# A written order for two more engines in a fused attention and feed-forward kernel

## The chip, the cores and the metric

The kernel runs on one NeuronCore of a Trainium2 chip. Five engines of the core work side by side, each through its own queue of instructions: TensorE (PE, matrix products; its weight loads are listed as PEld), VectorE (DVE), ScalarE (ACT), GpSimd (POOL) and SyncE (SP), which here only issues DMAs. Within a queue the instructions start in the order in which they stand; between queues semaphores hold an instruction back until what it needs is there. The metric is the device time of one execution in microseconds (us), lower is better.

## The reference

Eight batches of eight heads. Every head has 512 local tokens and 32 global ones, with 64 numbers each. The rows of all heads form x (4608 x 512), which goes through a feed-forward block.

```python
def _attn_ref(q_l, k_l, v_l, q_g, k_g, v_g):
    ...
    s_g = scale * np.matmul(q_g, k_all.transpose(0, 1, 3, 2))
    out_g = np.matmul(sm(s_g), v_all)                 # global queries see every key
    s_ll = np.where(mask, scale * np.matmul(q_l, k_l.transpose(0, 1, 3, 2)), -1e9)   # |i - j| <= 32
    s_lg = scale * np.matmul(q_l, k_g.transpose(0, 1, 3, 2))
    a_l = sm(np.concatenate([s_lg, s_ll], axis=-1))   # local queries: a band and the global keys
    out_l = np.matmul(a_l, np.concatenate([v_g, v_l], axis=2))
    return np.concatenate([out_g, out_l], axis=2)

def _moe_ref(x, w_in, w_out, s, b):
    r = np.maximum(x @ w_in, 0.0)                     # 512 -> 2048
    g = s * (r * r) + b
    return g @ w_out                                  # 2048 -> 512
```

## The kernel before

All work is written as one loop over 148 steps j. For j up to 127 a step computes the scores of one half of one head (256 local queries). Ten steps later, with m = j - 10, the feed-forward block works on the same data: 17 groups t of 256 rows (the last holds the global tokens), and for each group eight steps of 256 hidden columns, 136 steps m in all. So an ordinary step holds these pieces, in the order in which the loop writes them:

- `split(j + 1)` makes a rounded part and a remainder of the next keys and queries: two ScalarE copies (L191, L193) and two GpSimd subtractions (L192, L194). `load(j + 2)` puts the loads for a later step on SP.
- `scores(j)`: on TensorE the products `ps_s` (L350, one buffer) and, among them, the product of the global queries with these keys `ps_g` (L364; one buffer "g", shared with `ps_og` and `ps_tg` below). Then `softmax`: VectorE takes scores and mask and leaves the minimum (L207, twice), ScalarE takes two exponentials with their sums (L213), VectorE takes the reciprocal and scales (L216, L217, L222). Then `turn(j)`: VectorE copies the 16-bit halves apart (`two`, L385, four copies) and SP issues a DMA that transposes them (`turned`, L387). Last `g_sum(j)`: ScalarE copies one half of `ps_g` out (`tg`, L372), VectorE adds the other (`sg`, L373); this sets the buffer "g" free.
- `join(j - 1)`: a ScalarE copy that puts the turned halves together (`ptp`, L395). `two` and `turned` have one buffer each.
- `pv` on odd j only: 16 products of probabilities and values for two heads (L317) and a ScalarE copy of the result to x (L324).
- `ffn_in(m)`: 24 products (`ps_h`, L491, two buffers); relu on ScalarE (L497), square on VectorE (L498), the rounded part of g on ScalarE (L505), its remainder on VectorE (L506).
- `ffn_out(m - 1)`: 12 products (L524) with g of the step before. After each eighth m two copies `o` on ScalarE (L532) and their DMAs.

Some steps hold more. With j counted modulo 16: `x_split` after steps 9 and 1 (two ScalarE copies L462, two VectorE subtractions L463, from x to the operand `xs` of the next group, one buffer). The global heads come in steps 12 to 22, counted past 16 into the next batch: `g_softmax` (12 and 16), `g_transposes` inside `ffn_out` (15 and 19: five products L418, and for each of two parts a ScalarE copy L422 and a VectorE subtraction L423), `g_load` (15, 17, 19, 21: a load, two ScalarE copies L432, two GpSimd subtractions L433) and `g_pv` (16, 18, 20, 22: ten products L441, a ScalarE copy L445, VectorE sums L446 and L449).

The framework's planner settles the order inside each engine's queue from a model of its own: it takes instructions by priority (the order in which they are written) as they become ready in that model. From step 25 on (`ORDERED`), the block `tc.manual_schedule` makes TensorE's queue follow the written order exactly. ScalarE, VectorE, GpSimd and SP stay with the planner to the end.

Of the kernel before, what the change touches and what calls it, by code (L numbers as in the profile page):

```python
# [10 lines left out]
F32 = mybir.dt.float32  # L11
# [8 lines left out]
B, H, SL, SG, D = 8, 8, 512, 32, 64  # L20
DM, DF = 512, 2048
P = 128
# [22 lines left out]
NF = 16  # L45
# [10 lines left out]
G_TR = 3  # L56
G_LD = (0, 2)
# [10 lines left out]
def window_attention_then_ffn(ctx: ExitStack, tc: tile.TileContext, qd, qp, qg, kw, vw, vg, w_in, w_out, sv, bv, out):  # L68
# [4 lines left out]
    sb = ctx.enter_context(tc.tile_pool(name="sb", bufs=2))  # L73
# [94 lines left out]
    NS = B * 2 * H  # L168
    st_ = {}
# [24 lines left out]
        nc.gpsimd.tensor_sub(out=qs[:, 1, :], in0=rq, in1=f32(qs[:, 0, :]))  # L194
        st_["ks", j], st_["qs", j] = kq[:, 0:480], qs

    def softmax(heads, scores):
        hf = slot(heads[0])[1]
        nm = sb.tile([P, 4], F32, tag="nm", name=f"nm{heads[0]}")
        ss = sb.tile([P, 4], F32, tag="ss", name=f"ss{heads[0]}")[:, 0:2 * len(heads)]  # L200
        parts = []
        for j, p_s in zip(heads, scores):
            sm = st_["p", j] = sb.tile([P, NC], F32, tag="sm", name=f"sm{j}", bufs=4)
            for blk in range(2):
                n, c = len(parts), COLS[hf, blk]
                mask = masks[hf == 0 and blk == 0][:, 0:c.stop - c.start]
                nc.vector.tensor_tensor_reduce(  # L207
                    out=sm[:, c], in0=p_s[:, c], in1=mask,
                    op0=ALU.add, op1=ALU.min, scale=-scale, scalar=BIG, accum_out=nm[:, n:n + 1],
                )  # L210
                parts.append(sm[:, c])
        for n, p in enumerate(parts):
            nc.scalar.activation(  # L213
                out=p, in_=p, func=AF.Exp, bias=nm[:, n:n + 1], scale=-1.0, accum_out=ss[:, n:n + 1],
            )
        nc.vector.tensor_scalar_add(ss, ss, 1e-9)  # L216
        nc.vector.reciprocal(ss, ss)  # L217
        for n, p in enumerate(parts):
            if len(heads) == 2:
                nc.scalar.activation(out=p, in_=p, func=AF.Identity, scale=ss[:, n:n + 1])  # L220
            else:
                nc.vector.tensor_scalar(  # L222
                    out=p, in0=p, scalar1=ss[:, n:n + 1], scalar2=1.0, op0=ALU.mult, op1=ALU.mult,
                )
# [115 lines left out]
    def scores(j):  # L340
        b, hf, h = slot(j)
        ks, qs = st_.pop(("ks", j)), st_.pop(("qs", j))
        p_s = ps.tile([P, 512], F32, tag="s", name=f"ps_s{j}")
        late = j == ORDERED
        if not late:
            p_g = ps.tile([P, 512], F32, tag="g", name=f"ps_g{j}")
        for blk in range(2):
            cols = COLS[hf, blk]
            for a in range(2):
                nc.tensor.matmul(  # L350
                    p_s[:, cols], lhsT=qs[:, a, blk * P:(blk + 1) * P], rhs=ks[:, cols], start=(a == 0), stop=(a == 1),
                )
                if blk == hf and a == 0 and not late:
                    g_product(j, ks, p_g)
        softmax([j], [p_s])
        turn(j)
        if late:
            st_["late", j] = ks
        else:
            g_sum(j, p_g)  # L360

    def g_product(j, ks, p_g):
        b, hf, h = slot(j)
# [4 lines left out]
    def g_sum(j, p_g):  # L368
        b, hf, h = slot(j)
        ng = 256 + 32 * hf  # L370
        tg = sb.tile([P, 288], F32, tag="tg", name=f"tg{j}", bufs=1)
        nc.scalar.copy(out=tg[0:32, 0:ng], in_=p_g[32:64, 0:ng])  # L372
        nc.vector.tensor_add(out=sg_rows(j, 32)[:, hf * 256:hf * 256 + ng], in0=p_g[0:32, 0:ng], in1=tg[0:32, 0:ng])  # L373
# [7 lines left out]
    def turn(j):  # L381
        sm = st_.pop(("p", j)).bitcast(I16).rearrange("p (k h) -> p h k", h=2)
        two = sb.tile([P, 4, 2, P], I16, tag="two", name=f"two{j}", bufs=1)
        for blk, c, c0, q0, n, o in chunks(j):
            nc.vector.tensor_copy(out=two[:, 2 * blk + c], in_=sm[:, :, c0:c0 + P])  # L385
        turned = st_["turned", j] = sb.tile([P, 4, 2, P], I16, tag="turned", name=f"turned{j}", bufs=1)
        nc.sync.dma_start_transpose(  # L387
            turned.rearrange("p c h q -> p (c h) q"), two.rearrange("p c h k -> p (c h k)"),
        )
# [34 lines left out]
            yield  # L424

    def g_load(b, h):
        rv = sb.tile([P, 10 * D], F32, tag="rvg", name=f"rvg{b}_{h}", bufs=1)
        nc.sync.dma_start(rv, vg[b, h // 2])
        vs = sb.tile([P, 2, 5, 2, D], F32R, tag="vsg", name=f"vsg{b}_{h}", bufs=1)
        for i in range(2):  # L430
            rv5 = rv[:, 5 * D * i:5 * D * (i + 1)].rearrange("p (c d) -> p c d", d=D)
            nc.scalar.copy(out=vs[:, i, :, 0, :], in_=rv5)  # L432
            nc.gpsimd.tensor_sub(out=vs[:, i, :, 1, :], in0=rv5, in1=f32(vs[:, i, :, 0, :]))  # L433
        st_["vsg", b, h] = vs
# [44 lines left out]

    gs_ = {}  # L480

    def ffn_in(m):
        t, pr = m // 8, m % 8
        xs = xs_[t]
        p_h = ps.tile([P, 2, HALF], F32, tag="h", name=f"ps_h{m}", bufs=2)
        for k in range(2):
            f = 2 * pr + k
            n = 0
            for c in range(4):
                for a, e in ((0, 0), (0, 1), (1, 0)):  # L490
                    nc.tensor.matmul(  # L491
                        p_h[:, k], lhsT=wi[f][:, a, c, :], rhs=xs[:, e, c, :],
                        start=(n == 0), stop=(n == 11),
                    )
                    n += 1
        r = sb.tile([P, 2, HALF], F32, tag="r", name=f"r{m}", bufs=2)
        nc.scalar.activation(out=r, in_=p_h, func=AF.Relu)  # L497
        nc.vector.scalar_tensor_tensor(out=r, in0=p_h, scalar=s_t, in1=r, op0=ALU.mult, op1=ALU.mult)  # L498
        g = sb.tile([P, 2, 2, HALF], F32R, tag="g", name=f"g{m}")
        if GL_POOL(m):  # L500
            nc.vector.tensor_scalar_add(r, r, b_t)
            nc.scalar.copy(out=g[:, 0], in_=r)
            nc.gpsimd.tensor_sub(out=g[:, 1], in0=r, in1=f32(g[:, 0]))
        else:
            nc.scalar.activation(out=g[:, 0], in_=r, func=AF.Identity, bias=b_t)  # L505
            nc.vector.scalar_tensor_tensor(  # L506
                out=g[:, 1], in0=r, scalar=b_t, in1=f32(g[:, 0]), op0=ALU.add, op1=ALU.subtract,
            )
        gs_[m] = g
# [31 lines left out]
    nc.sync.dma_start(s_t, sv.partition_broadcast(P))  # L541
    nc.sync.dma_start(b_t, bv.partition_broadcast(P))

    NM = NT * 8
    extra, turns = defaultdict(list), {}
    for b in range(B):
        for g in range(2):
            s0 = 16 * b + G_AT[g]
            extra[s0].append(lambda b=b, g=g: g_softmax(b, g))
            turns[s0 + G_TR] = g_transposes(b, g)  # L550
            for i in range(2):
                h = 4 * g + 2 * i
                extra[s0 + G_TR + G_LD[i]].append(lambda b=b, h=h: g_load(b, h))
                extra[s0 + G_TR + G_PV[i]].append(lambda b=b, h=h: g_pv(b, h))

    def pick(pair, split_one):
# [18 lines left out]
    fixed = ExitStack()  # L575
    for j in range(NM + LAG + 2):
        if j == ORDERED:
            fixed.enter_context(tc.manual_schedule(engines={mybir.EngineType.PE}))
        sp(j + 1)
        if j + 4 < NF:  # L580
            ld(j + 4)
        if j + 2 >= NF:
            ld(j + 2)
        if NF <= j < NS and j % 2 == 0:
            v_load(j // 2)
        for _ in range(CHUNKS_AT[j] if j < len(CHUNKS_AT) else 0):
            weight_chunk(chunk)
            chunk += 1
        if j < NS:
            b1 = j // 16 + 1  # L590
            if j % 16 == 14 and b1 < B:
                qg_load(b1)
            sc(j)
            if j % 16 == 15 and NF <= j + 1 < NS:
                qg_split(b1)
        tr(j - 1)
        if NF <= j - 1 < NS:
            join(j - 1)
        pvs(j - 2)
        if NF <= j - 3 < NS and j % 2:  # L600
            pv((j - 3) // 2)
        if j == 0:
            vl32(0)
        vl32(j + 2)
        m = j - LAG
        if m == -1:
            x_split(0)
        if 0 <= m < NM:
            ffn_in(m)
            late_scores(j)  # L610
            if m % 8 == 7:
                t = m // 8 + 1
                if t < 16:
                    x_split(t)
                elif t == 16:
                    xg_split(16)
        for fn in extra.pop(j, []):
            fn()
        if 0 <= m - 1 < NM:
            ffn_out(m - 1, turns.pop(j, iter(())))  # L620
        else:
            list(turns.pop(j, ()))
    fixed.close()
    assert chunk == 16 and not extra


# [73 lines left out]
```

## Time and profile before

| | us |
|---|---|
| median of three runs | 1106.39 (1105.23 to 1108.20) |
| profiled execution | 1109.83 |
| its span, first to last instruction | 1108.0 |
| TensorE busy in the span | 998.3 |
| ScalarE busy | 748.3 |
| VectorE busy | 717.1 |
| GpSimd busy | 275.2 |

TensorE is at work for 90 per cent of the span. The first 190 us or so hold the loading of the weights and the steps up to 24, in the planner's order; then come about 800 us of steps with attention and feed-forward together; the last 100 us hold feed-forward steps alone. In the rows below, a line of a timeline gives the start and the length of a piece in us, the engine, the line, the operation, what it writes and reads, the shape, the number of instructions merged into it and, in brackets, how long the engine stood idle before it and what ended that.

### The profile page before, as it was taken

Reading aid. Unit: us, or ns where it says so; the run is one execution under the profiler, and the core shown is the slowest. Engines: PE = TensorE matmul, PEld = TensorE weight load, DVE = VectorE, ACT = ScalarE, POOL = GpSimd, SP = SyncE. Lnnn points to the kernel's source line nnn. Section 1 sums busy time; section 2 is a strip of 40 time slices with the busy share of each in tenths; the row PEclk is TensorE's granted clock in tenths of the full one; section 3 lists DMA queues with packets and bytes.
Section 4 is the critical chain, followed back from the end, with each engine's and each line's share of the span. In section 5 each row is a group of like instructions: output and inputs, shape, how many; then the busy total and the mean of one; then the engine's idle time right before and its main releaser. Section 6 shows DMA issues by size and latency. Waiting matters only on the chain.

```text
span 1108.0 us, 19924 instructions
## 1 busy us (share of the span) xinstructions
PE 998.3 (90%) x7060; PEld 877.7 (79%) x7060; DVE 717.1 (65%) x2092; ACT 748.3 (68%) x1618; POOL 275.2 (25%) x309
## 2 busy tenths in 40 slices
PE   6689996999899989989889889899899989999996
PEld 2378885988787778878779778888789878889995
DVE  6999566676666766766766666677666766664321
ACT  6987665777586766778667766778677766863221
POOL 0012323232322323223322332223322323201000
PEclk8879998999999999999999999899999999999998
DMA  9852443434443344434444454444344443331000
GB/s 325 311 198 51 110 100 95 102 87 107 110 113 83 90 115 103 103 85 122 109 91 99 98 110 92 104 85 128 80 109 100 104 117 83 82 57 46 11 20 19
DMA packets 179627, 115.07 MB, mean 104 GB/s; under 512 B 124744, under 2 KB 166728, under 8 KB 179528
## 3 DMA queue, kind: packets, MB, share of 16 engines
q1 hardware_dynamic: 179240, 112.76, 40.2%
q8 instruction: 55, 0.90, 0.4%
q10 hardware_dynamic: 288, 1.05, 0.4%
q14 instruction: 44, 0.36, 0.1%
HBM read 74.97 MB, written 9.44 MB: 76 GB/s over the span
## 4 chain that ended last, share of the span: by engine, by line
PE 22%; DMA 17%; ACT 12%; DVE 10%; issue 4%; POOL 0%; POOLq 0%; SPq 0%; ACTq 0%; DVEq 0%
DMA turned<-two 17%; PE ps_h L491 11%; PE acc L524 9%; ACT ptp L395 5%; DVE two L385 4%; ACT sm L213 3%; DVE sm L222 1%; DVE ss L216 1%; ACT kq L191 1%; DVE r L498 1%; ACT kq L193 1%; PE ps_op L317 1%; ACT tg L372 1%; PE ps_s L350 1%; DVE ss L217 1%
## 5 line engine op out<-in xcount | busy, mean ns | idle before, releaser
L491 PE MATMUL ps_h<-xs,w 128*128 128x256 f32 x3264 | 434.2, 289 | 16.3 <-DVE xs L463 10.1
L491 PEld LDWEIGHTS ps_h<-xs,w 128*128 128x128 f32 x3264 | 411.7, 196 | 27.9 <-DVE xs L463 11.9
L524 PE MATMUL acc<-w,g 128*128 128x512 f32 x1632 | 409.5, 398 | 0.4 <-ACT o L532 0.3
L524 PEld LDWEIGHTS acc<-w,g 128*128 128x128 f32 x1632 | 297.8, 190 | 60.6 <-DVE g L506 1.3
L192 POOL TENSOR_TENSOR kq<-rk,kq 64x416 fp32r<-64x416 f32 x112 | 122.8, 1097 | 614.3 <-ACT kq L191 607.9
L395 ACT COPY ptp<-turned 128x1024 int16<-128x1024 int16 x112 | 153.2, 1368 | 93.7 <-DMA turned<-two 93.3
L505 ACT ACTIVATE g<-r,b_t 128x512 fp32r<-128x512 f32 x136 | 98.4, 724 | 116.3 <-DVE r L498 116.2
L216 DVE TENSOR_SCALAR ss<-ss 128x2 f32<-128x2 f32 (+1 forms) x120 | 40.9, 341 | 169.3 <-ACT sm L213 169.1
L498 DVE SCALAR_TENSOR_TENSOR r<-ps_h,s_t,r 128x512 f32<-128x512 f32 x136 | 101.5, 746 | 74.2 <-ACT r L497 74.2
L385 DVE COPY two<-sm 128x256 int16<-128x256 int16 x448 | 132.9, 356 | 2.9 <-DMA turned<-two 2.7
L497 ACT ACTIVATE r<-ps_h 128x512 f32<-128x512 f32 x136 | 80.9, 595 | 75.2 <-PE ps_h L491 67.7
L506 DVE SCALAR_TENSOR_TENSOR g<-r,b_t,g 128x512 fp32r<-128x512 f32 x136 | 103.7, 763 | 40.5 <-ACT g L505 40.5
L213 ACT ACTIVATE sm<-sm,nm 128x224 f32<-128x224 f32 (+1 forms) x256 | 117.8, 462 | 3.0 <-DVE nm L207 3.0
L194 POOL TENSOR_TENSOR kq<-rq,kq 128x256 fp32r<-128x256 f32 x112 | 84.1, 751 | 13.7 <-POOL kq L192 2.9
L433 POOL TENSOR_TENSOR vsg<-rvg,vsg 128x320 fp32r<-128x320 f32 x64 | 59.7, 952 | 99.3 <-ACT vsg L432 99.3
L207 DVE CUSTOM_DVE_ANT_0 sm<-ps_s,mask 128x192 f32<-128x192 f32 (+1 forms) x224 | 74.1, 367 | 12.3 <-PE ps_s L350 12.2
L364 PE MATMUL ps_g<-kq,qgs 128*64 128x256 f32 (+1 forms) x112 | 33.9, 303 | 51.7 <-DVE og L446 32.2
L373 DVE TENSOR_TENSOR sg<-ps_g,tg 32x256 f32<-32x256 f32 (+1 forms) x112 | 48.3, 431 | 49.4 <-ACT tg L372 46.7
L350 PE MATMUL ps_s<-kq 128*128 128x192 f32 (+1 forms) x448 | 79.5, 267 | 0.0
L350 PEld LDWEIGHTS ps_s<-kq 128*128 128x128 f32 x448 | 72.3, 191 | 7.4 <-issue 0.3
L222 DVE TENSOR_SCALAR sm<-sm,ss 128x192 f32<-128x192 f32 (+1 forms) x224 | 68.6, 349 | 3.9
L317 PE MATMUL ps_op<-ptp,rvp 128*64 128x128 f32 (+2 forms) x1024 | 68.7, 268 | 2.0 <-ACT ptp L309 1.9
(68 smaller groups left out, 820.4 us busy)
## 6 DMA issues: line engine op xcount, KB each, us to landing
rvp<-in_vw SPq DMA_DIRECT2D x64, 256.0 KB, 3.1
rq<-in_qd SPq DMA_DIRECT2D x112, 128.0 KB, 2.4
rk<-in_kw SPq DMA_DIRECT2D x56, 208.0 KB, 2.4
rvg<-in_vg SPq DMA_DIRECT2D x32, 320.0 KB, 3.1
out<-o SPq DMA_DIRECT2D x34, 256.0 KB, 2.6
wst<-in_w_in SPq DMA_DIRECT2D x15, 512.0 KB, 6.5
wst<-in_w_out SPq DMA_DIRECT2D x15, 512.0 KB, 6.9
turned<-two SPq DMA_TRANSPOSE x112, 3.1
```

The costliest lines, as they stand in the source:

```text
L192: (nc.gpsimd if K_POOL(j) else nc.vector).tensor_sub(out=ks[p1:p1 + 64], in0=rk[p0:p0 + 64], in1=f32(ks[p0:p0 + 64]))
L194: nc.gpsimd.tensor_sub(out=qs[:, 1, :], in0=rq, in1=f32(qs[:, 0, :]))
L213: nc.scalar.activation(out=p, in_=p, func=AF.Exp, bias=nm[:, n:n + 1], scale=-1.0, accum_out=ss[:, n:n + 1],)
L350: nc.tensor.matmul(p_s[:, cols], lhsT=qs[:, a, blk * P:(blk + 1) * P], rhs=ks[:, cols], start=(a == 0), stop=(a == 1),)
L385: nc.vector.tensor_copy(out=two[:, 2 * blk + c], in_=sm[:, :, c0:c0 + P])
L395: nc.scalar.copy(out=pt.bitcast(I16).rearrange("p c (q h) -> p c h q", h=2), in_=st_.pop(("turned", j)))
L491: nc.tensor.matmul(p_h[:, k], lhsT=wi[f][:, a, c, :], rhs=xs[:, e, c, :], start=(n == 0), stop=(n == 11),)
L497: nc.scalar.activation(out=r, in_=p_h, func=AF.Relu)
L498: nc.vector.scalar_tensor_tensor(out=r, in0=p_h, scalar=s_t, in1=r, op0=ALU.mult, op1=ALU.mult)
L505: nc.scalar.activation(out=g[:, 0], in_=r, func=AF.Identity, bias=b_t)
L506: nc.vector.scalar_tensor_tensor(out=g[:, 1], in0=r, scalar=b_t, in1=f32(g[:, 0]), op0=ALU.add, op1=ALU.subtract,)
L524: nc.tensor.matmul(oacc[t][i], lhsT=g[:, a, k, i * P:(i + 1) * P], rhs=wo[f][:, e, :], start=(pr == 0 and n == 0), stop=(pr == 7 and n == 5),)
```

## The change

- `tc.manual_schedule` covers PE, Activation and DVE instead of PE alone: from step 25 on, ScalarE and VectorE also follow the written order. GpSimd and SP stay with the planner.
- The written order itself is edited. `g_sum` moves between the minima and the exponentials of `softmax`. `join(j - 1)` moves behind `pv`. In `ffn_in`, a list `then` of pieces runs between the products and the relu: `g_pv`, and `x_split` for the next group. So the activations of `ffn_in` come behind the copies and sums of `g_pv`, and behind `x_split`, in the queues of ScalarE and VectorE. `g_softmax` comes before `ffn_in`. `g_load` is cut in two: the load is written one step earlier than before, its copies (`g_split`) stand before `ffn_in`.

TensorE's written order stays as it was. No instruction is added or taken away.

```diff
-    def softmax(heads, scores):
+    def softmax(heads, scores, between=lambda: None):
...
+        between()
         for n, p in enumerate(parts):
             nc.scalar.activation(
...
-        softmax([j], [p_s])
-        turn(j)
         if late:
             st_["late", j] = ks
-        else:
-            g_sum(j, p_g)
+        softmax([j], [p_s], (lambda: None) if late else (lambda: g_sum(j, p_g)))
+        turn(j)
...
-        rv = sb.tile([P, 10 * D], F32, tag="rvg", name=f"rvg{b}_{h}", bufs=1)
+        rv = st_["rvg", b, h] = sb.tile([P, 10 * D], F32, tag="rvg", name=f"rvg{b}_{h}", bufs=1)
         nc.sync.dma_start(rv, vg[b, h // 2])
+
+    def g_split(b, h):
+        rv = st_.pop(("rvg", b, h))
         vs = sb.tile([P, 2, 5, 2, D], F32R, tag="vsg", name=f"vsg{b}_{h}", bufs=1)
...
-    def ffn_in(m):
+    def ffn_in(m, then):
...
+        for fn in then:
+            fn()
         r = sb.tile([P, 2, HALF], F32, tag="r", name=f"r{m}", bufs=2)
...
+    ENGINES = {getattr(mybir.EngineType, e) for e in ("PE", "Activation", "DVE")}
...
-            extra[s0].append(lambda b=b, g=g: g_softmax(b, g))
+            early[s0].append(lambda b=b, g=g: g_softmax(b, g))
...
-                extra[s0 + G_TR + G_LD[i]].append(lambda b=b, h=h: g_load(b, h))
+                early[s0 + G_TR + G_LD[i] - 1].append(lambda b=b, h=h: g_load(b, h))
+                early[s0 + G_TR + G_LD[i]].append(lambda b=b, h=h: g_split(b, h))
...
-            fixed.enter_context(tc.manual_schedule(engines={mybir.EngineType.PE}))
+            fixed.enter_context(tc.manual_schedule(engines=ENGINES))
...
-        if NF <= j - 1 < NS:
-            join(j - 1)
         pvs(j - 2)
         if NF <= j - 3 < NS and j % 2:
             pv((j - 3) // 2)
+        if NF <= j - 1 < NS:
+            join(j - 1)
...
+        for fn in early.pop(j, []):
+            fn()
...
+        then = extra.pop(j, [])
         if 0 <= m < NM:
-            ffn_in(m)
+            t = m // 8 + 1
+            if m % 8 == 7 and t < 16:
+                then.append(lambda: x_split(t))
+            ffn_in(m, then)
             late_scores(j)
-            if m % 8 == 7:
-                t = m // 8 + 1
-                if t < 16:
-                    x_split(t)
-                elif t == 16:
-                    xg_split(16)
-        for fn in extra.pop(j, []):
-            fn()
+            if m % 8 == 7 and t == 16:
+                xg_split(16)
```

## Rows read from the trace of the kernel before

**Rows 1.** The page: busy time, share of the span and instructions of each engine.
```profile
PE 998.3 (90%) x7060; PEld 877.7 (79%) x7060; DVE 717.1 (65%) x2092; ACT 748.3 (68%) x1618; POOL 275.2 (25%) x309
```

**Rows 2.** Stretches: length, busy PE PEld DVE ACT POOL, clock, DMA share, GB/s.
```profile
195.00:995.00 800.00, 735.51 (x5328) 658.86 (x5327) 532.51 (x1694) 571.84 (x1246) 229.80 (x252) 0.97 0.43 99
...
490.61:495.13 4.52, 4.52 (x29) 4.52 (x28) 2.32 (x9) 3.35 (x8) 1.81 (x2) 0.62 0.07 12
```

**Rows 3.** TensorE's waits, 195 to 995 us: us in total, times, longest.
```profile
PE ps_g L364 <- DVE og L446: 29.8, 22, 2.4
PE ps_g L364 <- DVE pg L423: 11.6, 7, 2.1
PE ps_h L491 <- DVE xs L463: 9.7, 7, 1.7
PE ps_og L441 <- DVE sg L373: 5.4, 5, 2.0
```

**Rows 4.** TensorE's timeline: an even and an odd step without global heads.
```profile
201.12 3.07 PE L491 MATMUL ps_h<-xs,w 128*128 128x256 f32 x24
204.03 2.94 PE L524 MATMUL acc<-w,g 128*128 128x512 f32 x12
...
207.34 2.99 PE L491 MATMUL ps_h<-xs,w 128*128 128x256 f32 x24
...
214.45 3.09 PE L491 MATMUL ps_h<-xs,w 128*128 128x256 f32 x24
```

**Rows 5.** TensorE's timeline: a long wait, and two blocks that ran slowly.
```profile
490.14 0.30 PE L364 MATMUL ps_g<-kq,qgs 128*64 128x256 f32 x1 [2.02 <-DVE pg L423]
...
490.61 4.52 PE L491 MATMUL ps_h<-xs,w 128*128 128x256 f32 x24
...
911.96 3.96 PE L491 MATMUL ps_h<-xs,w 128*128 128x256 f32 x24
```

**Rows 6.** ScalarE's timeline in two ordinary steps.
```profile
433.28 0.39 ACT L372 COPY tg<-ps_g 32x288 f32<-32x288 f32 x1
...
434.57 0.48 ACT L213 ACTIVATE sm<-sm,nm 128x224 f32<-128x224 f32 x1
...
435.60 0.60 ACT L497 ACTIVATE r<-ps_h 128x512 f32<-128x512 f32 x1
...
441.03 1.36 ACT L395 COPY ptp<-turned 128x1024 int16<-128x1024 int16 x1 [0.53 <-DMA turned<-two]
442.26 0.47 ACT L213 ACTIVATE sm<-sm,nm 128x224 f32<-128x224 f32 x1
...
442.85 0.37 ACT L324 COPY x<-ps_op 128x256 f32<-128x256 f32 x1
```

**Rows 7.** VectorE's timeline in one ordinary step.
```profile
437.02 0.90 DVE L385 COPY two<-sm 128x256 int16<-128x256 int16 x4
437.82 0.75 DVE L498 SCALAR_TENSOR_TENSOR r<-ps_h,s_t,r 128x512 f32<-128x512 f32 x1
```

**Rows 8.** VectorE's timeline, then GpSimd's, in a step with `g_load`.
```profile
403.85 2.24 DVE L385 COPY two<-sm 128x256 int16<-128x256 int16 x4
...
403.86 1.87 POOL L433 TENSOR_TENSOR vsg<-rvg,vsg 128x320 fp32r<-128x320 f32 x2 [0.76 <-ACT vsg L432]
```

**Rows 9.** TensorE's timeline around step 25, where its written order begins.
```profile
182.10 0.34 PE L364 MATMUL ps_g<-kq,qgs 128*64 128x288 f32 x1 [2.21 <-DVE sg L373]
187.95 0.50 PE L364 MATMUL ps_g<-kq,qgs 128*64 128x288 f32 x1 [5.50 <-DVE sg L373]
188.25 5.32 PE L524 MATMUL acc<-w,g 128*128 128x512 f32 x12
```

**Rows 10.** ScalarE by line, 195 to 995 us: count, busy, mean ns, idle before.
```profile
L395 ACT COPY ptp<-turned 128x1024 int16<-128x1024 int16 x102 | 139.5, 1368 | 82.4 <-DMA turned<-two 82.1
...
L505 ACT ACTIVATE g<-r,b_t 128x512 fp32r<-128x512 f32 x102 | 73.8, 724 | 97.3 <-DVE r L498 97.2
...
L432 ACT CAST vsg<-rvg 128x320 fp32r<-128x320 f32 x48 | 19.6, 455 | 0.0
```

More of the change, by code (lines that the diff above doesn't have):

```diff
@@ L542, in window_attention_then_ffn @@
     nc.sync.dma_start(b_t, bv.partition_broadcast(P))
+    ENGINES = {getattr(mybir.EngineType, e) for e in ("PE", "Activation", "DVE")}
     NM = NT * 8
-    extra, turns = defaultdict(list), {}
+    early, extra, turns = defaultdict(list), defaultdict(list), {}
     for b in range(B):
@@ L605, in window_attention_then_ffn @@
         m = j - LAG
+        for fn in early.pop(j, []):
+            fn()
         if m == -1:
             x_split(0)
+        then = extra.pop(j, [])
         if 0 <= m < NM:
-            ffn_in(m)
+            t = m // 8 + 1
+            if m % 8 == 7 and t < 16:
+                then.append(lambda: x_split(t))
+            ffn_in(m, then)
             late_scores(j)
-            if m % 8 == 7:
-                t = m // 8 + 1
-                if t < 16:
-                    x_split(t)
-                elif t == 16:
-                    xg_split(16)
-        for fn in extra.pop(j, []):
-            fn()
+            if m % 8 == 7 and t == 16:
+                xg_split(16)
+        else:
+            for fn in then:
+                fn()
         if 0 <= m - 1 < NM:
@@ L623, in window_attention_then_ffn @@
     fixed.close()
-    assert chunk == 16 and not extra
+    assert chunk == 16 and not extra and not early
 def kernel(**inputs):
```

## The prediction, made before the changed kernel was run

> **What bounds the kernel now.** I read the busy shares first [rows 1]: TensorE is busy for 90 per cent of the span, ScalarE for 68. Shares hide stages, so I then looked at the stretch in which all kinds of work run together, 195 to 995 us [rows 2]: TensorE is busy for 735.5 of 800 us and stands idle for 64.5. About 102 steps lie in it (the 102 joins and activations of rows 10), so a step takes 7.84 us there. The timeline of TensorE shows that steps without global heads have no gap: an even step takes 207.34 - 201.12 = 6.2 us, an odd one, with its `pv`, 7.1 us [rows 4]. The idle time is in the steps with global heads and with `x_split`, and the waits of TensorE say for whom [rows 3]: 29.8 us for `og` and 11.6 us for `pg`, both before the next `ps_g`, as they hold the one buffer "g"; 9.7 us for `xs`; 5.4 us for `sg`. The rest of the 64.5 us is small.
>
> There is a second price. After the wait of 2.02 us the next 24 products took 4.52 us, where 2.99 is usual [rows 4, 5]; the granted clock in that stretch was 0.62, so for part of it TensorE ran at 1.2 GHz and not at 2.4 [rows 2]. Eleven blocks of 24 between 237 and 916 us are slowed like this, each behind an idle wait of about 2 us or two waits close together; the one at 490 is among the slowest, the one at 912 the last [rows 5]. Set against 2.8 us for a block at full clock (2.9 from start to start in rows 4), they lose 16.6 us in all, 1.5 each. So waits of TensorE cost 64.5 + 16.6 = 81 us in this stretch, and that is the most that a better order of the other engines can give there.
>
> **Why TensorE waits.** The sums that free the buffer "g" are short, but the planner placed them late. ScalarE stands still before the joins for 82.4 us in total, 0.81 each, because the planner puts a join ahead of other ready work while the transposing DMA is still under way, and what frees "g" stands behind it [rows 10]. In the step of rows 8 the sums of `g_pv` also stand behind four copies `two` that took 2.24 us in place of 0.90 [rows 7, 8].
>
> **The change part by part.** I lay out each kind of step by the written order, with time 0 at the end of `scores(j)` on TensorE, and carry over how late ScalarE and VectorE come out of the step before. TensorE's own pieces: `pv` 0.9 (7.1 - 6.2), `ffn_in` 2.9 from start to start, `ffn_out` with the next scores 3.3 [rows 4]; I take 0.6 of that for the scores. A product of `ffn_in` starts every 0.12 us (2.9 / 24); I take 0.5 for the five of `g_transposes` and 0.7 for the ten of `g_pv`, which are smaller.
>
> *An ordinary step.* ScalarE's round is: `tg` and the two copies of a split 1.29 (433.28 to 434.57), exponentials 1.03, join 1.23 by its starts, relu 0.60 [rows 6], then it must wait 0.75 for the square on VectorE [rows 7], and the activation takes 0.72 [rows 10]: 5.6 us in even steps, 6.0 with the copy of x in odd ones [rows 6]. TensorE needs 6.2 and 7.1. So ScalarE keeps up and regains 0.6 and 1.1 us when it is late. The join now comes a full step after its DMA was issued, behind the exponentials: its wait of 0.81 goes. These steps did not hold TensorE up before, so this alone gives nothing; the cover is TensorE's own work.
>
> *`g_pv`, steps 16, 20, 22.* Its copy and sum are the first things behind `ffn_in` in both queues, while TensorE goes on with 2.8 us of `ffn_out` before it wants "g". In step 16 `g_softmax` stands in front: the copy ends at 5.2, the sum at 6.2, and the next `ps_g` is due at 6.4. The 29.8 us go. The relu, queued behind that copy, comes at most 2.5 us later than now; the remainder of g is then ready about 2 us into the next step and wanted at 2.9 or later. The waits for `sg` (5.4) go, because `g_sum` stands in front of the exponentials.
>
> *Step 15, `g_transposes`.* Exponentials end at 1.6, the copies for the next batch's queries and x at 2.2, the join at 3.4, `g_split` (two of 0.455, rows 10, overlapping a little) at 4.1, relu 4.7, square 5.5, g 6.3 (remainder 7.1), the copy of 128x512 out of "g" (as long as a relu) 6.9, its remainder on VectorE (as the square, but behind that of g) 7.75. TensorE is done with `ffn_out` at 7.1 and wants "g" at 7.2: it waits 0.6.
>
> *Step 17, `x_split`.* ScalarE is 1.8 late: join done at 4.7, `g_split` 5.5, the two copies `xs` 6.6, their VectorE halves 6.8 and 7.4. TensorE wants them at 7.1 and 7.8: nothing. If GpSimd is at `vsg` and holds VectorE up, 0.6. I take 0.3. In step 9 they are there by 5.7, so the 9.7 us go.
>
> *Step 18.* VectorE is 2.5 to 3 late, so `sg` frees "g" at 3.65 to 4.2, and `g_pv` is due at 2.9: a wait of 0.9. The two copies `o` now stand behind g in ScalarE's queue, the second behind the remainder of g, whose buffer it takes; `split` stands behind them.
>
> *Step 19, `g_transposes` again.* ScalarE is 2.25 late. The chain of step 15, without the queries' copy: exponentials 3.6, x 3.8, join 5.05, `g_split` 5.8, relu 6.4, square 7.2, g 7.9 (remainder 8.7), the copy 8.5, its remainder 9.4. "g" is wanted at 7.2: 2.2 us, and as behind the 2.02 us of rows 5, the clock then takes another 1.5.
>
> *Sum.* A batch loses 0.6 + 0.3 + 0.9 + 2.2 + 1.5 = 5.5 us, six batches 33. Single waits add 2: in step 26, where the sum of the late product of step 25 stands behind `x_split` (1.4), and before the last group (0.7). So 81 us of loss become 35: 46 gained.
>
> *GpSimd and SP* stay with the planner. The earlier load of `g_load` lands before `g_split` wants it; were it late, all of ScalarE's queue would stand. A load on SP in front of a `turned` DMA costs nothing while the join comes a step later. I take 0, with 0.8 us a join (its wait of today, rows 10) as the upper bound of a late landing.
>
> *Around step 25* TensorE now waits 2.21 and 5.50 us, then runs at half speed (5.32 against 2.8) [rows 4, 9]: 10.2 us. The sums it waits for stand ahead of more work in the new order, but steps up to 24 remain the planner's. Between -3 (one more wait as in step 19) and 10.2, I take 4, as only the second of the two waits lies behind work that the new order surely moves.
>
> Together 50 us. The profiled execution took 1109.8, 3.4 above the median: 1109.8 - 50 = 1060, and 1056 on the scale of the median.
>
> **The rivals.**
> 1. *GpSimd holds VectorE up* (1089). Four copies `two` took 2.24 us beside `vsg`, 0.90 alone [rows 7, 8]: 1.34 more. In a written order everything behind them waits as well. If that happens in each of the six steps 15 to 20, and the regained time covers half of it, TensorE waits another 4.0 us a batch and meets one more drop of the clock of 1.5: 6 x 5.5 = 33 more. Against it: in my layout `two` ends before `vsg` begins. The Trainium skill, SBUF — State Buffer, section "Who interferes with whom", says that VectorE in its two-port modes and GpSimd share a pair of ports that one of them holds for a whole instruction while the other is fully blocked. By that rule it is the order of issue that decides, and the change fixes VectorE's side of it alone; the trace agrees in that the copies waited and the GpSimd pair (1.87) ran through.
> 2. *ScalarE becomes the bound* (1115, slower). Its work is 571.8 us for 102 steps [rows 2], 5.6 each; with the wait for the square 6.4. TensorE's own, without the slow clock, is (735.5 - 16.6) / 102 = 7.05. If the joins still wait their 0.81 for the DMA, ScalarE is at 7.25, and a VectorE held up by 1.34 in every second step makes 7.92, more than today's 7.84: 8 us slower. The point from which it decides is 1.4 us of waits a step. Against it: the DMA has a step to land.
> 3. *It does not do what it says* (1105): the order written is what the planner already made, or new waits at the same places cost as much. The idle time before the joins speaks against the first.
> 4. *Nearly all waits vanish*, step 19's too, and step 25 is smooth: 1056 - 27 - 6 = 1023.
>
> **How the numbers follow.** The forecast has 0.60, with a range of its own from 1032 to 1080; rival 1 0.14, rival 2 0.13, rival 3 0.06, rival 4 0.07. The time is the forecast's, 1056. The range from 1021 to 1093 takes in the forecast and rivals 1 and 4, and leaves out rivals 2 and 3 (0.19). Faster by over 0.3 per cent, which is about what a measurement of this kernel can tell from none: 0.60 + 0.14 + 0.07 = 0.81; within it 0.06; slower 0.13.
>
> **What would show it.** Right: no wait of `ps_g` for `og` and few for `xs`; ScalarE's idle time before the joins near 0; one wait of about 2 us a batch for `pg`; TensorE idle for some 25 us in the stretch that 64.5 came from, with about six slow blocks. Wrong: ScalarE without idle time and TensorE waiting for g at `ffn_out` (rival 2); copies `two` of over 2 us in most global steps (rival 1); a join that waits for its DMA.

## The result, and the profile after

The changed kernel takes 1042.35 us (median of four runs, 1042.07 to 1043.26) against 1106.7 us beside it: a ratio of 0.942, 95% interval 0.940 to 0.944. It is 64 us faster, where 50 were forecast; the time lies in the range. The profiled execution took 1042.14 us, 67.7 less than that of before.

The gain can be placed, because TensorE runs the same 5310 products in the same order between the start of `ffn_out` in step 26 and its start in step 128 in both kernels. Here are the three stretches of before and of after (length, busy PE, PEld, DVE, ACT and POOL with their counts, granted clock, DMA share, GB/s).

```profile
173.50:196.90 23.40, 14.29 (x90) 12.08 (x89) 14.24 (x34) 13.26 (x30) 9.63 (x10) 0.78 0.33 81
196.90:994.51 797.61, 733.12 (x5310) 656.52 (x5309) 531.69 (x1693) 569.90 (x1240) 228.25 (x251) 0.97 0.43 100
994.51:1108.00 113.49, 104.69 (x698) 94.31 (x696) 35.35 (x50) 34.20 (x60) 5.27 (x6) 0.97 0.07 23
```

```profile
171.00:188.54 17.54, 14.58 (x100) 12.59 (x101) 13.42 (x43) 14.34 (x31) 3.63 (x4) 1.00 0.47 110
188.54:925.97 737.43, 709.75 (x5310) 640.65 (x5309) 508.85 (x1689) 571.96 (x1247) 232.49 (x256) 1.00 0.45 108
925.97:1040.30 114.33, 105.02 (x698) 94.31 (x696) 33.14 (x51) 33.72 (x59) 5.33 (x6) 0.97 0.07 23
```

`ffn_out` of step 26 is reached 8.4 us earlier (196.90 against 188.54), steps 26 to 128 take 60.2 us less (797.6 against 737.4), and the rest 0.8 more. In the middle stretch ScalarE has the same work as before, 572 us against 570. TensorE's idle time fell from 64.5 to 27.7 us, and its busy time, for the same products, from 733.1 to 709.8.

The waits of TensorE in that stretch (us in total, times, longest), which answer to [rows 3]:

```profile
PE ps_g L363 <- DVE pg L422: 20.2, 12, 2.2
PE ps_og L443 <- DVE sg L372: 6.0, 6, 1.1
PE ps_h L493 <- DVE xs L465: 1.4, 5, 0.3
```

The 29.8 us for `og` are gone and the 9.7 for `xs` nearly so. The 11.6 us for `pg` have become 20.2. And this is the group of the joins on the page of after, which answers to [rows 10]:

```profile
L394 ACT COPY ptp<-turned 128x1024 int16<-128x1024 int16 x112 | 152.7, 1363 | 6.2 <-DMA turned<-two 6.2
```

ScalarE stood still for 82.4 us before 102 joins; it now does so for 6.2 before all 112. The pattern of one batch, in TensorE's timeline, is four waits. They come at the same places in every batch, but the first batch lacks the one for `xs`, and the wait in step 15 goes from 0.55 us in the first batch to 1.56 in the last:

```profile
343.68 0.30 PE L363 MATMUL ps_g<-kq,qgs 128*64 128x256 f32 x1 [1.17 <-DVE pg L422]
...
358.80 2.97 PE L493 MATMUL ps_h<-xs,w 128*128 128x256 f32 x23 [0.26 <-DVE xs L465]
...
362.74 0.79 PE L443 MATMUL ps_og<-vsg,pg 128*64 128x128 f32 x10 [0.97 <-DVE sg L372]
...
376.37 0.33 PE L363 MATMUL ps_g<-kq,qgs 128*64 128x256 f32 x1 [2.19 <-DVE pg L422]
```

These are the waits that the layout in the prediction has in steps 15, 17, 18 and 19.

### The profile page after: what moved, and what is told of

Same layout as the page of the kernel before. It is cut to its first block, busy times and chain, and to the rows that moved or that the text cites. A ratio compares the mean times of both kernels' runs of the same rounds, so it can differ in the third digit from the quotient of the medians.

```text
span 1040.3 us, 19938 instructions
## 1 busy us (share of the span) xinstructions
PE 977.0 (94%) x7060; PEld 862.5 (83%) x7060; DVE 691.8 (66%) x2092; ACT 748.3 (72%) x1618; POOL 273.1 (26%) x309
## 5 line engine op out<-in xcount | busy, mean ns | idle before, releaser
L493 PE MATMUL ps_h<-xs,w 128*128 128x256 f32 x3264 | 421.1, 284 | 5.7 <-ACT xs L464 3.3
L493 PEld LDWEIGHTS ps_h<-xs,w 128*128 128x128 f32 x3264 | 399.0, 190 | 15.9 <-ACT xs L464 3.5
L528 PE MATMUL acc<-w,g 128*128 128x512 f32 x1632 | 404.2, 395 | 0.3 <-ACT g L509 0.2
L528 PEld LDWEIGHTS acc<-w,g 128*128 128x128 f32 x1632 | 294.8, 188 | 59.2 <-DVE g L510 1.1
L384 DVE COPY two<-sm 128x256 int16<-128x256 int16 x448 | 106.3, 300 | 0.1
L435 POOL TENSOR_TENSOR vsg<-rvg,vsg 128x320 fp32r<-128x320 f32 x64 | 55.7, 891 | 88.4 <-ACT vsg L434 88.4
L223 DVE TENSOR_SCALAR sm<-sm,ss 128x192 f32<-128x192 f32 (+1 forms) x224 | 66.2, 337 | 3.9
L217 DVE TENSOR_SCALAR ss<-ss 128x2 f32<-128x2 f32 (+1 forms) x120 | 32.8, 273 | 51.4 <-ACT sm L214 51.2
L318 PEld LDWEIGHTS ps_op<-ptp,rvp 128*64 128x64 f32 x1024 | 53.6, 140 | 13.0 <-issue 2.7
```

What stands on the lines that cost most here:

```text
L318: nc.tensor.matmul(p_o[64 * k:64 * k + 64, 0, blk, q0:q0 + n], lhsT=rv[:, k, v:v + D], rhs=pt[:, k, o] if i < NF // 2 else pt[:, k, 2 * bl ...
L493: nc.tensor.matmul(p_h[:, k], lhsT=wi[f][:, a, c, :], rhs=xs[:, e, c, :], start=(n == 0), stop=(n == 11),)
L528: nc.tensor.matmul(oacc[t][i], lhsT=g[:, a, k, i * P:(i + 1) * P], rhs=wo[f][:, e, :], start=(pr == 0 and n == 0), stop=(pr == 7 and n == 5),)
```

## The experiments

**Which half of the change does it.** The change binds two engines and edits the text. Theory A: the gain comes from the queues of ScalarE and VectorE following the written order, with the pieces at their new places. Rivals: the edited text alone does it through the planner's priorities (B), or the fixed order alone (C). The first two runs take one half each.

```diff
-    ENGINES = {getattr(mybir.EngineType, e) for e in ("PE", "Activation", "DVE")}
+    ENGINES = {getattr(mybir.EngineType, e) for e in ("PE",)}
```

> The written order of the changed kernel, but only TensorE has to follow it; ScalarE and VectorE are ordered by the planner again. Theory A (the gain comes from the queues of ScalarE and VectorE following the written order): the planner keeps putting joins in front of ready work and the sums that free the buffer g late, so 1085 to 1110 us, with ScalarE idle for over 60 us before the joins and TensorE waiting for og for over 15 us. Rival B (the edits of the text do it, since the planner takes them as priorities): 1040 to 1055 us, both waits near 0.

Measured: 1090.6 us, ratio 0.986 (0.982 to 0.990). The longest of TensorE's waits over the whole span, and ScalarE's group of the joins:

```profile
PE ps_g L363 <- DVE og L448: 23.0, 19, 2.4
```

```profile
L394 ACT COPY ptp<-turned 128x1024 int16<-128x1024 int16 x112 | 153.0, 1366 | 77.5 <-DMA turned<-two 77.0
```

As theory A has it: the joins still wait and the sums still come late under the planner, whatever the text. B falls; the text alone is worth 16 us.

The other half is the kernel before with

```diff
-            fixed.enter_context(tc.manual_schedule(engines={mybir.EngineType.PE}))
+            fixed.enter_context(tc.manual_schedule(engines={getattr(mybir.EngineType, e) for e in ("PE", "Activation", "DVE")}))
```

> The text of the kernel before, with ScalarE and VectorE bound to it from step 25 on, as TensorE is. Rival C (that both queues are fixed is enough, wherever the pieces stand): 1040 to 1055 us. Theory A holds the places to matter as well: g_sum behind the four copies costs nothing, as TensorE wants the buffer two microseconds later; but the sums of g_pv and the copies xs stand behind the four activations, which I lay out at 1 to 2.5 us of TensorE's waiting in each of the steps 9, 16, 17 and 18 of a batch: some 6 us a batch more than in the changed kernel, so 1070 to 1095 us, with waits for og and xs of 15 to 40 us. Joins wait for no DMA.

Measured: 1108.5 us, ratio 1.002 (1.000 to 1.004): no gain at all, more than 13 us above what was expected. TensorE's waits and the joins:

```profile
PE ps_og L441 <- DVE sg L373: 42.9, 26, 2.9
PE ps_tg L418 <- DVE sg L373: 17.9, 13, 2.4
```

```profile
L395 ACT COPY ptp<-turned 128x1024 int16<-128x1024 int16 x112 | 152.4, 1361 | 8.4 <-DMA turned<-two 8.3
```

C falls, and so does a part of my layout for this run. The joins no longer wait, as expected, yet nothing is won, because 61 us of waits for `sg` have come up. The waits for `og` and `xs`, expected at 15 to 40 us, are none and 10 us. I had held that `g_sum` behind the four copies costs nothing, since the next scores want the buffer "g" late. I had overlooked that `g_pv` and `g_transposes` of the same step want it right behind `ffn_in`.

**Which engine.** The next two runs bind one of the two engines, with the edited text.

```diff
-    ENGINES = {getattr(mybir.EngineType, e) for e in ("PE", "Activation", "DVE")}
+    ENGINES = {getattr(mybir.EngineType, e) for e in ("PE", "Activation")}
```

> The changed kernel, but VectorE is ordered by the planner; TensorE and ScalarE follow the written order. If the order of ScalarE alone carries the gain (the joins' idle 82 us are on ScalarE): 1042 to 1052 us. If each sum needs its place on both engines: 1055 to 1090 us, with TensorE waiting for VectorE's og or pg.

Measured: 1023.9 us, ratio 0.926 (0.922 to 0.931), which is 18 us less than with both. TensorE's one large wait from 188 us on:

```profile
PE ps_g L363 <- DVE pg L422: 14.6, 12, 1.9
```

Neither branch of the expectation held: with the edited text, the order of ScalarE carries the whole gain, and that of VectorE costs some. ScalarE alone bound with the old text was not run. The opposite run:

```diff
-    ENGINES = {getattr(mybir.EngineType, e) for e in ("PE", "Activation", "DVE")}
+    ENGINES = {getattr(mybir.EngineType, e) for e in ("PE", "DVE")}
```

> The changed kernel, but ScalarE is ordered by the planner; TensorE and VectorE follow the written order. If ScalarE's order carries the gain: 1085 to 1115 us, with over 60 us of ScalarE's idle time before the joins, now passed on to a VectorE that may not go ahead. If VectorE's order carries it: 1042 to 1060 us.

Measured: 1165.3 us, ratio 1.054 (1.049 to 1.058): slower, and by more than expected. TensorE's waits and the joins:

```profile
PE acc L528 <- ACT g L509: 35.9, 11, 5.7
PE ps_g L363 <- DVE pg L422: 30.2, 12, 3.7
```

```profile
L394 ACT COPY ptp<-turned 128x1024 int16<-128x1024 int16 x112 | 152.2, 1359 | 91.7 <-DMA turned<-two 91.2
```

The joins again wait 91 us, about as long as with neither engine bound (77 us, 1090.6 us), so the wait alone does not explain the loss; that VectorE now may not go round what the late ScalarE holds up is the likely reason. TensorE even waits for g before `ffn_out`, one of the two signs that the prediction named for its slower rival. The other, a ScalarE without idle time, is not there: it is busy for 745 of 1162 us.

**Which edit of the text.** With both engines bound as in the changed kernel, each of the next three runs takes one edit back. The places of `g_softmax` and of the two parts of `g_load` were not taken back by themselves.

```diff
-        softmax([j], [p_s], (lambda: None) if late else (lambda: g_sum(j, p_g)))
+        softmax([j], [p_s])
         turn(j)
+        if not late:
+            g_sum(j, p_g)
```

> The changed kernel, but g_sum stands behind the softmax and the four copies again. Theory A1: TensorE wants the buffer g not only for the next scores but 2.9 us after these for g_pv and g_transposes of the same step, and g_sum behind the copies ends at 3.7 or later, more when VectorE is late: 1090 to 1112 us with 45 to 65 us of waiting for sg. Rival: g_sum's place costs nothing, as I held when I forecast the run before: 1040 to 1048 us.

Measured: 1096.7 us, ratio 0.991 (0.988 to 0.994). TensorE's waits:

```profile
PE ps_og L445 <- DVE sg L374: 40.5, 24, 3.9
PE ps_tg L419 <- DVE sg L374: 17.8, 13, 2.4
```

The waits for `sg` are back, as expected. Taking back the place of `g_sum` alone loses 54 us of the 64 (1096.7 - 1042.4).

```diff
-        for fn in then:
-            fn()
         r = sb.tile([P, 2, HALF], F32, tag="r", name=f"r{m}", bufs=2)
...
         gs_[m] = g
+        for fn in then:
+            fn()
```

> The changed kernel, but the copies and sums of g_pv and x_split come behind the four activations of ffn_in, as in the text before. Theory A1 (after the run with the old text in a fixed order, which waited 61 us for sg and only 10 for xs, none for og): this edit is worth little, 1042 to 1056 us, with some 10 us more of waiting for xs. Rival: it is what makes the fixed order pay, 1065 to 1090 us with waits for og and xs of over 25 us.

Measured: 1044.5 us, ratio 0.944 (0.941 to 0.947). TensorE's waits:

```profile
PE ps_g L363 <- DVE og L448: 12.8, 6, 2.1
PE ps_g L363 <- DVE pg L422: 7.3, 12, 1.6
PE ps_h L493 <- DVE xs L465: 2.9, 13, 0.5
```

The time is as expected, the reason is not: 12.8 us of waits for `og` come back, all in step 16, and 12.9 us of those for `pg` go, probably because the relu and g no longer stand behind `g_pv` and the lateness carried to steps 15 and 19 is smaller. The edit only moves the loss to other steps; the waits for `xs` grow by 1.5 us, not by 10.

```diff
         tr(j - 1)
+        if NF <= j - 1 < NS:
+            join(j - 1)
         pvs(j - 2)
...
-        if NF <= j - 1 < NS:
-            join(j - 1)
```

> The changed kernel, but join stands before pv and its copy again. Theory A: behind the exponentials it waits for no DMA either way, only the copy of x comes 1.2 us later, and nothing waits for that: 1040 to 1045 us. Rival (the place of the join is a part of the gain): over 1050 us.

Measured: 1041.7 us, ratio 0.941 (0.938 to 0.944). As expected, the move of the join past `pv` is worth nothing. In a fixed order it stands behind the exponentials in both texts, and ScalarE stands still for 6.6 us before all 112 joins here.

**What the waits that are left come from.** The waits for `pg` in steps 15 and 19 were laid out as the cost of a copy that stands behind the four activations. This run puts it ahead of them. It also moves the fifth product of `g_transposes` on TensorE, from between the halves of `ffn_out` to ahead of both.

```diff
-        then = extra.pop(j, [])
+        turn_ = turns.pop(j, iter(()))
+        then = [lambda: next(turn_, None)] + extra.pop(j, [])
...
-            ffn_out(m - 1, turns.pop(j, iter(())))
+            ffn_out(m - 1, turn_)
```

> The changed kernel, but in steps 15 and 19 the first products of g_transposes, and with them the copy and the remainder that free g, come right behind the products of ffn_in, ahead of the relu. If the waits for pg in steps 15 and 19 come from the place behind the four activations (20.2 us in 12 waits): they fall below 3 us, and with them the drops of the clock: 1015 to 1026 us. If the relu, now later, makes TensorE wait for g instead: 1035 to 1050 us.

Measured: 1024.2 us, ratio 0.926 (0.923 to 0.929). No wait for `pg` is left, and no drop of the clock between step 26 and the end of the products. What TensorE still waits for is

```profile
PE ps_og L443 <- DVE sg L372: 6.1, 6, 1.1
PE ps_g L363 <- DVE og L448: 4.9, 6, 1.0
```

The next question is why VectorE's written order costs 18 us against the planner's. In the changed kernel ScalarE's exponentials of the global heads wait for their maximum, which stands behind the four copies on VectorE, and in the run with ScalarE alone bound this wait is missing from the list of ScalarE's waits:

```profile
ACT sg L405 <- DVE gm L404: 19.3, 14, 1.5
```

```diff
+        if j % 16 == G_AT[0] and j // 16 < B:
+            g_max(j // 16, 0)
+        if j % 16 == G_AT[1] % 16 and 0 <= (j - G_AT[1]) // 16 < B:
+            g_max((j - G_AT[1]) // 16, 1)
         if j < NS:
...
     def g_softmax(b, g):
...
-        nc.vector.reduce_max(out=gm, in_=v, axis=mybir.AxisListType.X)
-        nc.vector.tensor_scalar_mul(gm, gm, -scale)
```

> The changed kernel, but the maximum of g_softmax is taken at the start of its step, ahead of the scores' softmax, and not behind the four copies. Theory V (VectorE's written order costs 18 us against ScalarE's alone because ScalarE's exponentials of the global heads wait for that maximum, 19.3 us in 14 waits, and the delay is carried to the waits for sg and pg): 1024 to 1034 us, that wait of ScalarE below 5 us, TensorE's waits for sg near 0 and for pg below those 20.2 us. Rival W (it is the remainder of pg, which VectorE may not take before the remainder of g): 1038 to 1044 us, with ScalarE's wait gone and TensorE's waits for pg as they are.

Measured: 1032.1 us, ratio 0.932 (0.930 to 0.934). ScalarE's wait for the maximum, and then TensorE's waits:

```profile
ACT sg L409 <- DVE gm L403: 0.5, 1, 0.5
```

```profile
PE ps_g L363 <- DVE pg L426: 16.9, 12, 2.2
PE ps_og L447 <- DVE sg L372: 1.4, 6, 0.3
```

So this one place explains 10 of the 18 us. The next run makes both edits together, the maximum early and the transposes' copy ahead of the relu; these are their main lines:

```diff
+        then = [lambda: next(turn_, None)] + extra.pop(j, [])
...
+            g_max(j // 16, 0)
```

> The changed kernel with both: the maximum of g_softmax at the start of its step, and the first part of g_transposes ahead of the relu. By theory V, which says the two remove different waits: 1008 to 1020 us, TensorE idle for less than 5 us from step 26 to step 128. By W the second does nothing on top: 1022 to 1027 us, as with the transposes alone.

Measured: 1016.6 us, ratio 0.918 (0.916 to 0.920), in the range of theory V. TensorE's waits for `sg` in step 18 are back at 6.2 us, though, and TensorE stands idle for 6.8 us from step 26 to step 128 where less than 5 were expected, so the two do not add up cleanly. The last run leaves VectorE to the planner and moves the transposes' copy.

```diff
-    ENGINES = {getattr(mybir.EngineType, e) for e in ("PE", "Activation", "DVE")}
+    ENGINES = {getattr(mybir.EngineType, e) for e in ("PE", "Activation")}
...
+        then = [lambda: next(turn_, None)] + extra.pop(j, [])
```

> ScalarE in the written order and VectorE with the planner, as in the run at 1023.9 us, and the first part of g_transposes ahead of the relu. That run still waited 14.6 us for pg, 12 times. If the place of the copy on ScalarE is the cause: those waits go, 1005 to 1015 us. If the planner puts the remainder late on VectorE: 1018 to 1026 us.

Measured: 1008.5 us, ratio 0.910 (0.908 to 0.913), the fastest kernel of this study. From step 26 on TensorE waits for nearly nothing:

```profile
PE ps_og L443 <- DVE sg L372: 0.6, 1, 0.6
PE ps_h L493 <- DVE xs L479: 0.5, 1, 0.5
```

The copy's place on ScalarE was the cause, not the planner's place for the remainder. The 8 us between this run and the one before it lie in the stretch from step 26 to step 128, which took 711.1 us there and 702.5 here: 6.2 us are idle time of TensorE, mostly the waits for `sg`, and 2.5 are busy time for the same products. Which instruction of VectorE the planner places better was not followed.

## Why the prediction was right

**The layout of the steps held.** Step 19 is the one it was worked out for in full: a wait of 2.2 us, and 2.2 were measured. Here are ScalarE's timeline and then VectorE's in that step; time 0 of the layout is 366.8, the end of the scores.

```profile
369.54 0.45 ACT L214 ACTIVATE sm<-sm,nm 128x192 f32<-128x192 f32 x1
...
370.84 1.38 ACT L394 COPY ptp<-turned 128x1024 int16<-128x1024 int16 x1
372.07 0.82 ACT L434 CAST vsg<-rvg 128x320 fp32r<-128x320 f32 x2
372.78 0.61 ACT L501 ACTIVATE r<-ps_h 128x512 f32<-128x512 f32 x1
374.21 0.72 ACT L509 ACTIVATE g<-r,b_t 128x512 fp32r<-128x512 f32 x1 [0.82 <-DVE r L502]
374.84 0.73 ACT L421 CAST pg<-ps_tg 128x512 fp32r<-128x512 f32 x2
```

```profile
373.42 0.75 DVE L502 SCALAR_TENSOR_TENSOR r<-ps_h,s_t,r 128x512 f32<-128x512 f32 x1 [0.83 <-ACT r L501]
374.96 0.75 DVE L510 SCALAR_TENSOR_TENSOR g<-r,b_t,g 128x512 fp32r<-128x512 f32 x1 [0.79 <-ACT g L509]
375.63 0.88 DVE L422 TENSOR_TENSOR pg<-ps_tg,pg 128x512 fp32r<-128x512 f32 x2
```

Relu starts at 6.0 (5.8 in the layout), the square is ready at 7.4 (7.2), g is done at 8.1 (7.9), and TensorE's `ps_g` starts at 9.6 (9.4). The other steps: 0.6 laid out for step 15 and 1.2 measured in the usual batch; 0.3 and 0.26 for step 17; 0.9 and 0.97 for step 18. A batch waits 4.6 us where 4.0 were expected, and the stretch 27.7 us in all. The 0.7 before the last group was a wait of 0.5 us for `xs`, in a stretch behind step 128 that became 0.8 us longer.

**Three terms of the sum were mis-sized.** The forecast was 50 us and the profiled executions lie 67.7 apart; the kernel got faster than laid out, so it is the range that holds, not the sum. Steps 26 to 128 gained 60.2 us; the layout had 48 (81 less 33). Idle time went from 64.5 to 27.7 us, 3.7 less of a gain than the 40.5 that six batches of 4.0 would have given. The rest, 23.4 us, is TensorE's busy time for the same products, where the sum had 7.6 (16.6 less 9).

First, the price of the clock after the change: one drop in each of six batches was taken, two came. Second, the 81 us had left out what the view of busy time hides besides the slow blocks. The two traces tell them apart if each product is measured up to the start of the next, without idle time, and set against the mean of its kind at full clock. The products that started at the low clock took 19.0 us more in the kernel before and 2.8 in the changed one, which is 16.2 us of the 23.4; 12.8 of these lie in the blocks of 24, and the rest in other products. (The prediction's 16.6 us for the blocks before is 15.0 by this measure; against the 2.8 us a block that it names, its eleven blocks would have lost about 18.) The last product before a wait is recorded longer than the time to the next start elsewhere, as 0.25 us at 373.93, before the wait of 2.19, where 0.12 is usual, and so counts a part of the wait as busy: 8.6 us before and 3.6 after, another 5.1. About 2 us were not placed.

**Step 25**, the third term, gave 8.4 us up to the start of `ffn_out` in step 26, where 4 less the 1.4 of step 26 had been forecast. The 4 was a choice between two bounds, -3 and 10.2, and not laid out. Of the two waits of [rows 9], both before a `ps_g`, the one of 2.21 us is gone and the one of 5.50 is now 2.44; a new one of 0.47 stands before the next `ps_g`, where the layout had 1.4 us. The half-speed products behind the waits are at full speed:

```profile
178.70 0.30 PE L363 MATMUL ps_g<-kq,qgs 128*64 128x288 f32 x1
...
181.56 0.34 PE L363 MATMUL ps_g<-kq,qgs 128*64 128x288 f32 x1 [2.44 <-DVE sg L372]
181.75 2.91 PE L528 MATMUL acc<-w,g 128*128 128x512 f32 x12
...
185.44 0.35 PE L363 MATMUL ps_g<-kq,qgs 128*64 128x288 f32 x1 [0.47 <-DVE sg L372]
```

So the first wait went too, though the prediction held only the second to be surely moved; 0.9 of the 8.4 us were won even ahead of `ffn_in` in step 25 (its first product starts at 176.79 before and at 175.91 after).

**The reason given for `sg` was right in the sum and incomplete in its cause.** The prediction booked 5.4 us for `g_sum` in front of the exponentials. In the kernel before that was all, since the planner mostly placed it early enough. In a fixed order the same edit decides over 54 us, as the run without it shows. The prediction never weighed the order without the edits; of the two halves of the change alone, the text is worth 16 us and the order nothing, and together they are worth 64.

**The rivals.** Rival 1 (GpSimd holding VectorE up) did not come: the four copies of a step got shorter. This is their group on the page of before and then on that of after.

```profile
L385 DVE COPY two<-sm 128x256 int16<-128x256 int16 x448 | 132.9, 356 | 2.9 <-DMA turned<-two 2.7
```

```profile
L384 DVE COPY two<-sm 128x256 int16<-128x256 int16 x448 | 106.3, 300 | 0.1
```

The copies take 27 us less in all. In step 19 of the batch shown above they run from 371.69 to 372.58 us, between GpSimd's subtractions for the next keys and queries, which end at 370.96, and `vsg`, which begins at 372.61: the order that the layout had.

```profile
371.69 0.89 DVE L384 COPY two<-sm 128x256 int16<-128x256 int16 x4
...
372.61 1.71 POOL L435 TENSOR_TENSOR vsg<-rvg,vsg 128x320 fp32r<-128x320 f32 x2 [1.65 <-ACT vsg L434]
```

The Trainium skill, SBUF — State Buffer, section "Who interferes with whom", says that the order of issue decides which of the two engines is held up. The trace agrees: in the kernel before, the 56 copies that began while a GpSimd subtraction ran took 0.85 us each, and the 17 that a subtraction joined later took 0.285, as did the 375 that met none; in the changed kernel only 10 began under one. It is ScalarE's order that brought this about, where the prediction put it down to VectorE's: with ScalarE alone bound the copies take 300 ns as well, with VectorE alone bound 341. GpSimd's `vsg` waits for a copy of ScalarE, as in the line above, so the place of that copy sets when the two can meet.

Rival 2 (ScalarE as the bound, joins still waiting) came in half when VectorE alone was bound: 1165 us, the joins at 91 us of waiting, but ScalarE idle for a third of the span, so it was not the bound. Its price in the prediction also rests on a slip: by its rows 5.6, 0.75 and 0.81 us are 7.17 a step and not 7.25, and with 0.67 more 7.84, which is today's step and no loss. In the changed kernel the joins came a step behind their DMA, as argued against it. Rival 3 falls with the result, rival 4 asked for the waits of step 19 to go, and they did not.

## What to carry to other kernels

When an engine that everything waits for stands idle, ask which short instruction frees its buffer and where that one stands in the queues of the engines between; the place of a sum of 0.4 us was worth 54 here. Here a fixed order paid only together with the right places, and not on every engine: bind the queue whose planner misjudges a wait (a DMA here), and try leaving the others free. Laying a step out by hand from the trace's own durations, with the lateness carried from step to step, was good to 0.2 us for the step in which it was worked out in full.

## What the runs showed of the hardware

The same wait of TensorE does not always cost clock. In the kernel before, twelve drops to 1.2 GHz from step 26 to step 128 began during or soon after a wait of about 2 us or more (ten) or the second of two waits of 1.1 to 1.7 us close together (two), but three waits of 2.02 to 2.35 us had none. In the changed kernel six waits of 2.18 to 2.22 us, at the same place of six batches, came with two drops. These are the two stretches, with the clock at 0.50:

```profile
259.11:262.53 3.42, 3.42 (x16) 3.42 (x17) 1.93 (x10) 2.45 (x7) 1.66 (x2) 0.50 0.43 126
723.33:726.74 3.41, 3.16 (x15) 3.16 (x16) 1.92 (x10) 2.41 (x8) 1.80 (x2) 0.50 0.42 133
```

The same place had one drop for six waits of 2.2 us in the run with the join ahead of `pv`, and three in the run with the maximum early. What tells such a wait with a drop from one without was not tried.
